# One projection burst and one transpose group per pair of heads, in an attention-plus-FFN kernel

## The chip, the core and the metric

The kernel runs on one core of one Trainium2 chip. The metric is the device time of one execution in microseconds (us). Each version is timed in several runs, and the median is compared. One further execution is recorded by the hardware profiler; its span runs from the first instruction to the last.

## The reference

A linear attention feeds a feed-forward network (FFN). All data are fp32.

```python
def phi(x):
    proj = np.einsum('bhsd,df->bhsf', x, w_phi)
    proj = proj - np.max(np.abs(proj), axis=-1, keepdims=True)
    return np.concatenate([np.exp(proj), np.exp(-proj)], axis=-1)
q_p, k_p = (phi(q), phi(k))
kv = np.einsum('bhsf,bhsd->bhfd', k_p, v)
z = np.sum(k_p, axis=2)
num = np.einsum('bhsf,bhfd->bhsd', q_p, kv)
den = np.einsum('bhsf,bhf->bhs', q_p, z)[..., None] + 1e-06
...
h = x @ w_in
g = np.maximum(h, 0.0) + alpha * np.minimum(h, 0.0)
return (g @ w_out).astype(np.float32)
```

There are 8 x 8 heads of 576 tokens with 64 dimensions, and 128 projected features, so phi has 256. The FFN sees 4608 tokens, 512 model dimensions and 2048 hidden ones.

## The kernel before

Two heads at a time form a pair, 32 pairs in all, numbered 0 to 31. One head lies on partitions 0 to 63, the other on 64 to 127. A pair goes through these steps, each a function inside `attention_units`:

- `project(0)` (L307) projects the first 512 tokens of k, 16 matmuls with a 64-row contraction into a two-bank PSUM tile `pj`. `project(1)` does the tails (the last 64 tokens of k and of q share a tile, one small PSUM tile `pl` for each head) and then the first 512 tokens of q into `pj`. There is one `pj` buffer. VectorE (DVE) follows with a maximum (L311, tile `m`) and a subtraction (L312, tile `t`) for each piece; these two are called the shift of that piece.
- `k_exp` takes exp of both signs on ScalarE (ACT): `xk` (L325) of the 512 tokens, `k` (L320) of the tail.
- `k_z` (L365) sums k features by multiplying with ones, `k_acc` (L348) accumulates `kv`, both into one PSUM bank `kv`. `kv_out` (L375) copies it to `ks`.
- `kv_turn` (L380, three transposes into `kt`) and `q_turn` (L391 for the tails, L394 for the rest, ten transposes into `qt`) turn kv and q; `kv_copy` (L384) and `q_exp` (L402, L404) bring them to SBUF as `sf` and `qf`.
- `den` (L431) and `num` (L413) multiply `qf` with `sf` into the PSUM tiles `d` and `n`; ACT copies them out (L441, L424). The denominator goes through DRAM to be inverted on DVE (L450) and spread, GpSimd multiplies, and the result is stored to `x_d`.

The FFN goes in two passes over the hidden dimension. The first five of sixteen hidden blocks are done beside the attention, one chunk of 512 tokens at a time (`ffn1_units`): four steps of three matmuls (L503 to L505) make one hidden block `h`; ACT makes `r` and `g` from it (L235, L236), DVE joins them (L240), ACT casts `gh` (L123), DVE makes the rest `gl` (L127), and steps of three matmuls (L509 to L511) multiply down into `o`, which ACT copies to `os` (L554). The second pass follows once all attention is done, at about 630 us. Weights come as 64-bit words and are decoded in blocks during the attention: ACT scales (L173), DVE splits in four instructions (L181 to L184, tiles `aw` and `ew`), GpSimd adds, ACT casts (L123, `raww`), GpSimd subtracts.

The order of the instructions on TensorE (PE), SyncE, DVE and ACT is written by hand: every step is a unit with a place on a time axis, on which one pair takes 1.0, and all units are emitted sorted by place. `places(i)` holds the places of pair i relative to i, `decode_at` those of the weight decoding, `ffn1_units` those of the FFN. The engines run their instructions in that order; places are no times. Pairs 0 to 8 (`ZP = 9`) are called early here. No FFN lies beside them but at the end, and z is made by 20 PE instructions from `xk`. For the later pairs DVE adds up z (L334, L338, L341), and 10 or 11 FFN steps lie within each. A cycle begins at the tail projection of its pair, and the start of that instruction is called T0.

Of the kernel before, what the change touches and what calls it, by code (L numbers as in the profile page):

```python
# [8 lines left out]
F32 = mybir.dt.float32  # L9
# [3 lines left out]
ALU = mybir.AluOpType  # L13
# [3 lines left out]
P = 128  # L17
# [22 lines left out]
WA = (0.0040, 0.50)  # L40
# [17 lines left out]
def places(i):  # L58
# [3 lines left out]
        ld=-1.90,  # L62
        lv=-0.80,
        p=(-0.9955 if early else -0.993, 0.0),
        ke=(-0.26, 0.0011),
        ks=(0.0015, 0.0022, 0.0026),
        kz=1.0002,
        ka=1.0012,
        ko=1.0025,
        kr=1.10,  # L70
        kc=1.16,
        q=(1.34, 1.50, 1.20),
        qe=(1.46, 1.62, 1.28),
        d=2.0004,
        ds=2.0008,
        n=2.005,
        s=2.0055,
# [31 lines left out]
def fused_kernel(ctx: ExitStack, tc: tile.TileContext, kq, v, w_phi, w_in, w_out, alpha, out):  # L109
# [111 lines left out]
    def decode_at(t, blk):  # L221
        return [(t + (WT if t < TL else WL)[k], lambda u=u: u(*blk, WN)) for k, u in stages.items()]
# [32 lines left out]
    ps_m = ps_m_.enter_context(tc.tile_pool(name="ps_m", bufs=3, space=PSUM))  # L255
# [5 lines left out]
    ps_pj = att.enter_context(tc.tile_pool(name="ps_pj", bufs=1, space=PSUM))  # L261
# [3 lines left out]
    pool.memset(ones, 1.0)  # L265
    k4buf = []
# [5 lines left out]
    def attention_units(i):  # L272
# [12 lines left out]
        def project(ch):  # L285
            t = c["t", ch] = wk.tile([P, 2, 4 + ch, FD], F32, tag=f"t{ch}", name=f"t{i}_{ch}", bufs=1 + ch)
            dst, out, js = {}, [], [0, 1, 2, 3]
            if ch:
                js = [4] + js
                for h in range(2):  # L290
                    p1 = ps_m.tile([P, 1, 1, FD], F32, tag="m", name=f"pl{i}_{h}")
                    dst[h, 4] = p1[:, 0, 0]
                    out.append((slice(h, h + 1), slice(4, 5), p1))
            if ch == 0 and i < 2:
                for h in range(2):
                    p1 = psf.tile([P, 1, 4, FD], F32, tag="f", name=f"pj{i}_{ch}_{h}")
                    dst.update({(h, j): p1[:, 0, j] for j in range(4)})
                    out.append((slice(h, h + 1), slice(0, 4), p1))
            else:
                p2 = ps_pj.tile([P, 2, 4, FD], F32, tag="pj", name=f"pj{i}_{ch}")  # L300
                dst.update({(h, j): p2[:, h, j] for h in range(2) for j in range(4)})
                out.append((slice(0, 2), slice(0, 4), p2))
            for j in js:
                for h in range(2):
                    hs = slice(h * D, (h + 1) * D)
                    ts = slice((4 * ch + j) * P, (4 * ch + j + 1) * P)
                    pe.matmul(dst[h, j], lhsT=c["raw"][hs, ts], rhs=w_sb[hs], start=True, stop=True)  # L307
            for n, (hs, js, src) in enumerate(out):
                nh, nj = hs.stop - hs.start, js.stop - js.start
                m = wk.tile([P, nh, nj], F32, tag="m", name=f"m{i}_{ch}_{n}", bufs=4)  # L310
                dve.tensor_reduce(m, src, axis=AX.X, op=ALU.max, apply_absolute_value=True)  # L311
                dve.tensor_tensor(  # L312
                    t[:, hs, js], src, m.unsqueeze(3).broadcast_to([P, nh, nj, FD]), op=ALU.subtract
                )
# [28 lines left out]

        def k_acc():
# [11 lines left out]
        def k_z():  # L356
            c["kv"] = ps_kv.tile([P, 3, FD], F32, tag="kv", name=f"kv{i}")
# [15 lines left out]
        def kv_out():  # L373
            c["ks"] = st.tile([P, 3, FD], F32, tag="ks", name=f"ks{i}", bufs=1)
            act.copy(c["ks"], c["kv"])  # L375

        def kv_turn():
            ps = c["kt"] = ps_m.tile([P, 3, P], F32, tag="m", name=f"kt{i}")
# [422 lines left out]
```

## Time and profile before

| | us |
|---|---|
| median of 3 runs | 1140.08 (1139.42 to 1140.46) |
| profiled execution, its own time | 1140.04 |
| its span | 1138.2 |
| PE busy | 1114.4 (98%) |
| DVE busy | 634.0 (56%) |
| ACT busy | 561.1 (49%) |

1.84 us of the profiled execution lie outside its span. Lines L12 are those of the kernel. In a timeline row stand start, time of the instruction or of the group, engine, line, operation, result tile <- operand tiles, shapes, count, and in brackets the idle time ahead of it with what ended it. On PE the form `64*128` is the part of the array in use (rows by columns). Matmuls overlap, so what one costs is read from the start of it to the start of the next.

### The profile page before, as it was taken

The numbers are of one execution on the slowest core, as the hardware profiler recorded it, in microseconds if no ns is written. First come the engines' busy times: TensorE is split into PE (matmuls) and PEld (weight loads), VectorE is DVE, ScalarE is ACT, GpSimd is POOL, SyncE is SP. The second block draws the span as 40 slices with busy tenths as digits, with TensorE's granted clock in tenths as the row PEclk, the third lists the DMA queues.
The fourth block names the chain that finished last, engine by engine and source line by source line (L and its number), as shares of the span: only waits on it lengthen the run. The fifth ranks groups of instructions, "written<-read, shape, count | busy, mean of one in ns | idle before, by whom it ended". The sixth has DMA issues, their size and how long they took to land.

```text
span 1138.2 us, 18351 instructions
## 1 busy us (share of the span) xinstructions
PE 1114.4 (98%) x7232; PEld 865.2 (76%) x7232; DVE 634.0 (56%) x978; ACT 561.1 (49%) x1149; POOL 213.9 (19%) x219
## 2 busy tenths in 40 slices
PE   6999999999999999999999999999999999999998
PEld 5766767777777777677778788888888888888886
DVE  7888957798687777836861342424242333333322
ACT  4777656666666765664543333333333333433332
POOL 1345332322424142243542000000000000000000
PEclk9999999999999999999999999999999999999999
DMA  5467264555556365466627030303030302112021
GB/s 190 147 186 219 68 194 143 172 164 183 162 167 195 99 211 167 146 202 219 227 65 246 32 111 1 111 1 111 1 111 1 111 1 75 37 33 79 1 74 37
DMA packets 74101, 133.68 MB, mean 117 GB/s; under 512 B 14624, under 2 KB 24480, under 8 KB 73376
## 3 DMA queue, kind: packets, MB, share of 16 engines
q1 hardware_dynamic: 71712, 122.48, 33.7%
q0 software_dynamic: 2016, 9.96, 2.5%
q8 instruction: 57, 0.93, 0.3%
q14 instruction: 28, 0.23, 0.1%
q10 hardware_dynamic: 288, 0.07, 0.0%
HBM read 93.92 MB, written 38.42 MB: 116 GB/s over the span
## 4 chain that ended last, share of the span: by engine, by line
PE 88%; DVE 6%; DMA 4%; ACT 2%; issue 1%; SPq 0%; DVEq 0%; ACTq 0%
PE h L503 11%; PE h L505 11%; PE h L504 11%; PE po L511 8%; PE po L509 8%; PE po L510 8%; PE kv L348 6%; PE n L413 5%; PE pj L307 5%; PE o L511 3%; PE o L509 3%; PE o L510 3%; PE d L431 2%; PE qt L394 2%; DMA xr<-x_d 2%; PE kv L365 1%
## 5 line engine op out<-in xcount | busy, mean ns | idle before, releaser
L240 DVE SCALAR_TENSOR_TENSOR g<-r,aln,g 128x512 f32<-128x512 f32 x144 | 111.7, 775 | 307.1 <-ACT g L236 306.9
L235 ACT ACTIVATE r<-h 128x512 f32<-128x512 f32 x144 | 86.5, 601 | 293.3 <-PE h L505 293.2
L127 DVE TENSOR_TENSOR gl<-g,gh 128x512 fp32r<-128x512 f32 x144 | 104.7, 727 | 67.6 <-ACT gh L123 67.1
L123 ACT CAST gh<-g 128x512 fp32r<-128x512 f32 x144 | 90.0, 625 | 85.6 <-DVE g L240 85.6
L236 ACT ACTIVATE g<-h 128x512 f32<-128x512 f32 x144 | 86.0, 598 | 1.0 <-DMA part_d<-os 1.0
L509 PE MATMUL po<-gh,wd 128*128 128x512 f32 x216 | 84.6, 392 | 0.7 <-ACT gh L123 0.7
L510 PE MATMUL po<-gh,wd 128*128 128x512 f32 x216 | 84.7, 392 | 0.0
L511 PE MATMUL po<-gl,wd 128*128 128x512 f32 x216 | 84.5, 391 | 0.0
L311 DVE TENSOR_REDUCE m<-pj 128x8 f32<-128x1024 f32 (+1 forms) x66 | 78.2, 1185 | 10.4 <-PE pj L307 10.3
L307 PE MATMUL pj<-w_sb,raw 64*128 64x128 f32 x1024 | 73.2, 283 | 9.8 <-DMA w_sb<-w_phi_dram 4.6
L307 PEld LDWEIGHTS pj<-w_sb,raw 64*128 64x128 f32 x1024 | 64.1, 192 | 23.3 <-issue 15.6
L189 POOL TENSOR_TENSOR aw<-ew,aw 128x256 f32<-128x256 f32 x64 | 56.6, 885 | 128.6 <-DVE ew L184 128.6
L312 DVE TENSOR_TENSOR t<-pj,m 128x1024 f32<-128x1024 f32 (+1 forms) x66 | 78.7, 1192 | 2.3
L509 PE MATMUL o<-gh,w 128*128 128x512 f32 x180 | 76.0, 422 | 2.6 <-ACT os L554 2.4
L463 POOL TENSOR_TENSOR s<-s,rr 128x576 f32<-128x576 f32 x32 | 48.5, 1517 | 145.3 <-DMA rr<-rec_d 127.7
L503 PE MATMUL h<-xh,w 128*128 128x512 f32 x180 | 75.8, 421 | 0.0
L511 PE MATMUL o<-gl,w 128*128 128x512 f32 x180 | 71.7, 399 | 3.6 <-DVE gl L127 3.4
L404 ACT ACTIVATE qf<-qt 128x512 f32<-128x512 f32 x128 | 68.4, 615 | 6.3 <-PE qt L394 6.3
L511 PE MATMUL po<-gl,w 128*128 128x512 f32 x180 | 69.7, 390 | 1.4 <-DVE gl L127 1.4
L505 PE MATMUL h<-xl,w 128*128 128x512 f32 x180 | 70.7, 393 | 0.0
L510 PE MATMUL o<-gh,w 128*128 128x512 f32 x180 | 70.6, 392 | 0.0
L504 PE MATMUL h<-xh,w 128*128 128x512 f32 x180 | 70.5, 392 | 0.0
(105 smaller groups left out, 2402.6 us busy)
## 6 DMA issues: line engine op xcount, KB each, us to landing
xr<-x_d SPq DMA_DIRECT2D x18, 1024.0 KB
raw<-kq_dram SPq DMA_DIRECT2D x31, 576.0 KB
v<-v_dram SPq DMA_DIRECT2D x32, 320.0 KB
w_d<-raww SPq DMA_DIRECT2D x38, 256.0 KB
rr<-rec_d SPq DMA_DIRECT2D x64, 144.0 KB
x_d<-s SPq DMA_DIRECT2D x32, 288.0 KB
part_d<-os SPq DMA_DIRECT2D x36, 256.0 KB
pt<-part_d SPq DMA_DIRECT2D x9, 1024.0 KB
```

The lines of the kernel that those rows point to most:

```text
L123: return act.copy(dst, src)
L127: return eng.tensor_tensor(dst, src, f(hi), op=ALU.subtract)
L235: act.activation(st["r"], ps, AF.Relu, scale=-1.0)
L236: act.activation(st["g"], ps, AF.Relu)
L240: dve.scalar_tensor_tensor(g, st["r"], aln[:, ff : ff + 1], g, op0=ALU.mult, op1=ALU.add)
L307: pe.matmul(dst[h, j], lhsT=c["raw"][hs, ts], rhs=w_sb[hs], start=True, stop=True)
L503: pe.matmul(ps, lhsT=wt[0][:, ws], rhs=xh, start=n == 0, stop=False)
L504: pe.matmul(ps, lhsT=wt[1][:, ws], rhs=xh, start=False, stop=False)
L505: pe.matmul(ps, lhsT=wt[0][:, ws], rhs=xl, start=False, stop=n == NK - 1)
L509: pe.matmul(ps, lhsT=wt[2][:, ws], rhs=gh, start=first, stop=False)
L510: pe.matmul(ps, lhsT=wt[3][:, ws], rhs=gh, start=False, stop=False)
L511: pe.matmul(ps, lhsT=wt[2][:, ws], rhs=gl, start=False, stop=last)
```

## The change

On PE the pieces of a pair's cycle get another order. The three projections stand together at its start as one burst of nine tiles: the tails, the first 512 tokens of k of the next pair, the first 512 tokens of q. Behind them come, in later pairs, kv, the numerator, the denominators and z; in early pairs the denominators, z, kv and the numerator. All transposes of a pair form one group, in later pairs behind the first FFN step, where before they stood in four places between FFN steps: three of kv, two of the q tails, eight of q. The q tails are turned from the lower 64 partitions alone (`t[D:P]`), 64 columns each, beside the turned kv in one PSUM bank `kq`.

PSUM is divided anew: `pj` has two buffers, shared by the projections, the turned q and the numerator, where `ps_m` has one buffer instead of three. The tail of the first head is projected into a free column of the bank in which kv of the pair before is accumulated afterwards (`kvb`). The shifts are units of their own (`shift`), in the order tail of head 0, next pair's k, tail of head 1, q. On ACT, `xk` moves to place -0.45, `qf` is made by one instruction for each sign in later pairs, and the numerator is copied out by one. The second decode block of an early pair is taken right behind the first. A split whose place falls late in a cycle (over .88) moves behind the shifts of the next one.

The core of the diff:

```diff
-WA = (0.0040, 0.50)
+WA = (0.0040, 0.0046)
...
-        ld=-1.90,
+        ld=-1.9988,
...
-        p=(-0.9955 if early else -0.993, 0.0),
-        ke=(-0.26, 0.0011),
...
+        p=(-0.9994 if i < ZP + 3 else -0.9998, 0.0004),
...
+        ke=(-0.45, 0.0014),
...
     def decode_at(t, blk):
-        return [(t + (WT if t < TL else WL)[k], lambda u=u: u(*blk, WN)) for k, u in stages.items()]
+        us = []
+        for k, u in stages.items():
+            at = t + (WT if t < TL else WL)[k]
+            if k == "split" and ZP < at < TL and at % 1 > 0.88:
+                at = int(at) + 1.0009
+            us.append((at, lambda u=u: u(*blk, WN)))
+        return us
...
-    ps_m = ps_m_.enter_context(tc.tile_pool(name="ps_m", bufs=3, space=PSUM))
+    ps_m = ps_m_.enter_context(tc.tile_pool(name="ps_m", bufs=1, space=PSUM))
...
-    ps_pj = att.enter_context(tc.tile_pool(name="ps_pj", bufs=1, space=PSUM))
+    ps_pj = att.enter_context(tc.tile_pool(name="ps_pj", bufs=2, space=PSUM))
...
+        def shift(n):
+            ch, hs, js, src = c["p", n]
...
+            dve.tensor_reduce(m, src, axis=AX.X, op=ALU.max, apply_absolute_value=True)
+            dve.tensor_tensor(
+                c["t", ch][:, hs, js], src, m.unsqueeze(3).broadcast_to([P, nh, nj, FD]), op=ALU.subtract
+            )
...
+        def project(ch, js):
+            if len(js) == 1:
+                kvb[i] = ps_kv.tile([P, 4, FD], F32, tag="kv", name=f"kv{i}")
+                pl = ps_m.tile([P, 4, FD], F32, tag="m", name=f"pl{i}")
+                dst = [kvb[i][:, 3:4], pl[:, 0:1]]
...
+            else:
+                dst = ps_pj.tile([P, 2, 4, FD], F32, tag="pj", name=f"pj{i}_{ch}")
...
+        def kv_bank():
...
+            c["kv"] = kvb[i + 1]
...
+        def q_turn():
+            for g in range(2):
+                pe.transpose(c["kq"][:, 3, g * D : (g + 1) * D], c["t", 1][D:P, g, 0, :], ident[D:P, D:P])
...
         def num():
+            c["n"] = ps_pj.tile([P, 2, 512], F32, tag="pj", name=f"n{i}")
...
-        for n in range(2):
-            us.append((at["p"][n], lambda n=n: project(n)))
+        us.append((at["p"][0], lambda: project(0, range(4))))
+        us.append((1.0008, kv_bank))
+        us.append((at["pl"], lambda: project(1, range(1))))
+        us.append((at["p"][1], lambda: project(1, range(1, 5))))
+        for n in range(4):
+            us.append((at["sh"][n], lambda n=n: shift(n)))
```

The order of PE at the start of pair 21's cycle, before: `pl21` are its tails, `pj21_1` its q, `pj22_0` the k of pair 22; `kv20` belongs to pair 20, `d19` and `n19` to pair 19.

```order
L307 MATMUL pl21_0_3868<-w_sb_73,raw21_3578 128x128
L307 MATMUL pl21_1_3869<-w_sb_73,raw21_3578 128x128
L307 MATMUL pj21_1_3870<-w_sb_73,raw21_3578 128x128 x8
L365 MATMUL kv20_3890<-z20_3727,ones_119 32x128 x4
L431 MATMUL d19_3895<-qf19_3793,sf19_3772 32x288 x8
L348 MATMUL kv20_3890<-xk20_3653,v20_3591 64x256 x8
L348 MATMUL kv20_3890<-k4_0_121,v20_3591 64x256 x2
L413 MATMUL n19_0_3928<-qf19_3793,sf19_3772 64x288 x4
L413 MATMUL n19_1_3933<-qf19_3793,sf19_3772 64x288 x4
L307 MATMUL pj22_0_3942<-w_sb_73,raw22_3767 128x128 x8
L503 MATMUL h1_3_2_3850<-xh1_3_3571,w2_92 128x512
L504 MATMUL h1_3_2_3850<-xh1_3_3571,w2_92 128x512
```

The same place now; `kv21` is the bank that takes the first tail of pair 21 and then kv of pair 20.

```order
L320 MATMUL kv21_3740<-w_sb_73,raw21_3420 128x128
L320 MATMUL pl21_3741<-w_sb_73,raw21_3420 128x128
L320 MATMUL pj22_0_3744<-w_sb_73,raw22_3605 128x128 x8
L320 MATMUL pj21_1_3753<-w_sb_73,raw21_3420 128x128 x8
L359 MATMUL kv21_3740<-xk20_3527,v20_3491 64x256 x8
L359 MATMUL kv21_3740<-k4_0_121,v20_3491 64x256 x2
L432 MATMUL n19_3798<-qf19_3667,sf19_3662 64x288 x8
L449 MATMUL d19_3807<-qf19_3667,sf19_3662 32x288 x8
L375 MATMUL kv21_3740<-z20_3643,ones_119 32x128 x4
L525 MATMUL h1_3_2_3728<-xh1_3_3462,w2_92 128x512
L526 MATMUL h1_3_2_3728<-xh1_3_3462,w2_92 128x512
L527 MATMUL h1_3_2_3728<-xl1_3_3463,w2_92 128x512
```

The projection of pair 22's k stood behind the numerator and now stands ahead of kv; the denominators and z stood ahead of kv and now stand behind the numerator.

The order of DVE ahead of that burst, before: L240 joins an FFN block, L450 inverts, L127 makes the rest, L181 to L184 split a weight block, L311 and L312 are the shifts.

```order
L240 SCALAR_TENSOR_TENSOR g1_3_0_3800<-r1_3_0_3799,aln_76,g1_3_0_3800 128x512
L450 RECIPROCAL r9_18_3847<-d9_18_3791 128x9
L127 TENSOR_TENSOR gl1_3_0_3854<-g1_3_0_3800,gh1_3_0_3834 128x512
L240 SCALAR_TENSOR_TENSOR g1_3_1_3840<-r1_3_1_3839,aln_76,g1_3_1_3840 128x512
L181 TENSOR_SCALAR aw8_0_0_3832<-aw8_0_0_3832 128x256
L182 SCALAR_TENSOR_TENSOR aw8_0_0_3832<-raww8_0_0_3786,aw8_0_0_3832 128x256
L183 TENSOR_SCALAR ew8_0_0_3857<-aw8_0_0_3832 128x256
L184 SCALAR_TENSOR_TENSOR ew8_0_0_3857<-raww8_0_0_3786,ew8_0_0_3857 128x256
L311 TENSOR_REDUCE m21_1_0_3881<-pl21_0_3868 128x1
L312 TENSOR_TENSOR t21_1_3867<-pl21_0_3868,m21_1_0_3881 128x128
L311 TENSOR_REDUCE m21_1_1_3884<-pl21_1_3869 128x1
L312 TENSOR_TENSOR t21_1_3867<-pl21_1_3869,m21_1_1_3884 128x128
```

DVE now, at the same place (L248 is the join, L468 the reciprocal, L129 the rest, L300 and L301 the shifts):

```order
L248 SCALAR_TENSOR_TENSOR g1_3_0_3691<-r1_3_0_3690,aln_76,g1_3_0_3691 128x512
L468 RECIPROCAL r9_18_3725<-d9_18_3684 128x9
L129 TENSOR_TENSOR gl1_3_0_3732<-g1_3_0_3691,gh1_3_0_3715 128x512
L248 SCALAR_TENSOR_TENSOR g1_3_1_3721<-r1_3_1_3720,aln_76,g1_3_1_3721 128x512
L300 TENSOR_REDUCE m21_0_3763<-kv21_3740 128x1
L301 TENSOR_TENSOR t21_1_3762<-kv21_3740,m21_0_3763 128x128
L300 TENSOR_REDUCE m22_2_3767<-pj22_0_3744 128x8
L301 TENSOR_TENSOR t22_0_3766<-pj22_0_3744,m22_2_3767 128x1024
L300 TENSOR_REDUCE m21_1_3770<-pl21_3741 128x1
L301 TENSOR_TENSOR t21_1_3762<-pl21_3741,m21_1_3770 128x128
L300 TENSOR_REDUCE m21_3_3773<-pj21_1_3753 128x8
L301 TENSOR_TENSOR t21_1_3762<-pj21_1_3753,m21_3_3773 128x2x512
```

The split of weight block 8 has moved from ahead of the shifts to behind them, the shift of pair 22's k stands between the two tails, and the join of FFN block 1 (`g1_3_1`) is still ahead of all of them.

The order of ACT ahead of that burst, before: L235 and L236 make r and g, L404 the q features, L123 casts, L173 scales, L325 makes `xk`.

```order
L235 ACTIVATE r1_3_0_3799<-h1_3_0_3758 128x512
L236 ACTIVATE g1_3_0_3800<-h1_3_0_3758 128x512
L404 ACTIVATE qf19_3793<-qt19_0_3803 128x512 x2
L404 ACTIVATE qf19_3793<-qt19_1_3818 128x512 x2
L123 CAST raww7_1_256_3634<-aw7_1_256_3667 128x256
L173 ACTIVATE aw8_0_0_3832<-raww8_0_0_3786 128x256
L123 CAST gh1_3_0_3834<-g1_3_0_3800 128x512
L235 ACTIVATE r1_3_1_3839<-h1_3_1_3810 128x512
L236 ACTIVATE g1_3_1_3840<-h1_3_1_3810 128x512
L325 ACTIVATE xk21_3843<-t21_0_3745 128x1024 x2
L441 ACTIVATE ds19_3904<-d19_3895 128x288
L320 ACTIVATE k4_1_123<-t21_1_3867 64x256 x2
```

ACT now (L243 and L244 are r and g, L423 the q features, L125 the casts, L175 the scale, L331 `xk`):

```order
L419 ACTIVATE qf19_3667<-kq19_3647 128x2x64 x2
L423 ACTIVATE qf19_3667<-qt19_3653 128x2x512
L243 ACTIVATE r1_3_0_3690<-h1_3_0_3639 128x512
L244 ACTIVATE g1_3_0_3691<-h1_3_0_3639 128x512
L423 ACTIVATE qf19_3667<-qt19_3653 128x2x512
L331 ACTIVATE xk21_3706<-t21_0_3582 128x1024 x2
L125 CAST raww7_1_256_3521<-aw7_1_256_3552 128x256
L175 ACTIVATE aw8_0_0_3713<-raww8_0_0_3679 128x256
L125 CAST gh1_3_0_3715<-g1_3_0_3691 128x512
L243 ACTIVATE r1_3_1_3720<-h1_3_1_3697 128x512
L244 ACTIVATE g1_3_1_3721<-h1_3_1_3697 128x512
L326 ACTIVATE k4_1_123<-t21_1_3762 64x256 x2
```

`xk21`, which stood behind r and g of FFN block 1, now stands ahead of them, and so ahead of the cast and scale of the weights and of `gh` too.

121 lines of the change are left out of this document (56 added, 65 removed).

## The prediction

> **What bounds the kernel now.** I read the page first, then the groups of waits of PE, then the timelines of PE, DVE and ACT around single pairs.
>
> ```profile
> PE 1114.4 (98%) x7232; PEld 865.2 (76%) x7232; DVE 634.0 (56%) x978; ACT 561.1 (49%) x1149; POOL 213.9 (19%) x219
> ...
> PE o L509 <- ACT os L554: 2.4, 1, 2.4
> PE d L431 <- ACT qf L404: 1.0, 2, 0.7
> ```
>
> PE is busy 98% of the span, so a change can gain only where PE does the same work in less time or waits less, and it loses where PE is made to wait. What its work costs stands in the timeline of PE around pair 21, whose cycle begins at T0 = 309.31 (start, length, line):
>
> ```profile
> 308.99 0.39 PE L505 MATMUL h<-xl,w 128*128 128x512 f32 x1
> 309.31 0.49 PE L307 MATMUL pl<-w_sb,raw 64*128 64x128 f32 x4
> 309.63 1.06 PE L307 MATMUL pj<-w_sb,raw 64*128 64x128 f32 x16
> 310.62 0.42 PE L365 MATMUL kv<-z,ones 128*32 128x128 f32 x8
> ...
> 311.95 1.95 PE L348 MATMUL kv<-xk,v 128*64 128x256 f32 x16
> ...
> 314.16 2.11 PE L413 MATMUL n<-qf,sf 128*64 128x288 f32 x16
> 316.20 1.16 PE L307 MATMUL pj<-w_sb,raw 64*128 64x128 f32 x16
> 317.29 0.50 PE L503 MATMUL h<-xh,w 128*128 128x512 f32 x1
> ...
> 318.08 0.49 PE L380 MATMUL kt<-ident,ks 128*128 128x128 f32 x3
> ...
> 319.11 0.38 PE L391 MATMUL qt<-ident,t 128*128 128x128 f32 x2
> ...
> 320.72 0.60 PE L394 MATMUL qt<-ident,t 128*128 128x128 f32 x4
> ...
> 321.85 0.60 PE L394 MATMUL qt<-ident,t 128*128 128x128 f32 x4
> ```
>
> From start to start the tails take 0.32 us, the q projection 0.99, z and denominators 1.33, kv 2.21, the numerator 2.04, the next k projection 1.09. Nowhere here does PE wait. The four-transpose group and the FFN step behind it take 1.13 (320.72 to 321.85), the three-transpose group and its step 1.03 (318.08 to 319.11), so a transpose is 0.10 to 0.11 and a step 0.69 to 0.71, and a group has no price of its own.
>
> DVE is 56% busy, but in bursts. Its timeline around the same T0:
>
> ```profile
> 309.59 0.75 DVE L240 SCALAR_TENSOR_TENSOR g<-r,aln,g 128x512 f32<-128x512 f32 x1 [0.29 <-ACT g L236]
> 310.26 0.29 DVE L181 TENSOR_SCALAR aw<-aw 128x256 uint32<-128x256 uint32 x1
> ...
> 311.78 0.28 DVE L311 TENSOR_REDUCE m<-pl 128x1 f32<-128x128 f32 x1
> 312.10 0.29 DVE L312 TENSOR_TENSOR t<-pl,m 128x128 f32<-128x128 f32 x1
> 312.31 0.28 DVE L311 TENSOR_REDUCE m<-pl 128x1 f32<-128x128 f32 x1
> ...
> 312.83 1.21 DVE L311 TENSOR_REDUCE m<-pj 128x8 f32<-128x1024 f32 x1
> 314.08 1.22 DVE L312 TENSOR_TENSOR t<-pj,m 128x1024 f32<-128x1024 f32 x1
> ```
>
> A join (L240) takes 0.67, a split of weights 1.52, the shift of one tail 0.53, that of a 1024-column piece 1.25 and 1.22. I call S the start of the first tail's shift; here it is T0 + 2.47, since a join and a split lie ahead of it, and PE doesn't care. It begins to care at pair 29:
>
> ```profile
> 442.08 0.49 PE L307 MATMUL pl<-w_sb,raw 64*128 64x128 f32 x4
> ...
> 446.93 2.11 PE L413 MATMUL n<-qf,sf 128*64 128x288 f32 x16
> 449.19 1.16 PE L307 MATMUL pj<-w_sb,raw 64*128 64x128 f32 x16
> 445.61 0.28 DVE L311 TENSOR_REDUCE m<-pl 128x1 f32<-128x128 f32 x1
> 447.91 1.22 DVE L312 TENSOR_TENSOR t<-pj,m 128x1024 f32<-128x1024 f32 x1
> ```
>
> S is T0 + 3.53 there. The subtraction that frees the only `pj` buffer ends at 449.13, and the next projection starts 0.06 later, 2.26 behind the numerator's start instead of 2.04. So before, the kernel bore an S of about T0 + 3.3 without loss.
>
> **PE's own work.** In later pairs the next k projection moves beside the q projection. A projection behind another kind of matmul costs 1.09, and 0.99 is what q takes with only the exit from this form; so an entry and an exit, 0.10 each, go away: -0.20 a pair. The transposes gather in one group, which by the above saves nothing; but the two tails are now turned on 64 rows, in the midst of 128-row transposes. No such transpose is in the trace. From below, they cost half a transpose each and no change of form: -0.1 a pair. From above, they take a whole 0.11 each, and the array changes form twice, at the exit and entry prices that the projections show (leaving transposes +0.09, into 64 rows +0.10, out +0.10, into transposes +0.05): +0.35. For the first, the leaving price, early pairs show it:
>
> ```profile
> 52.85 0.55 PE L380 MATMUL kt<-ident,ks 128*128 128x128 f32 x3
> ...
> 54.42 0.49 PE L307 MATMUL pl<-w_sb,raw 64*128 64x128 f32 x4
> ...
> 63.42 0.55 PE L380 MATMUL kt<-ident,ks 128*128 128x128 f32 x3
> ```
>
> The 13 transposes there last 1.57 up to the first projection, 0.15 more than 13 times 0.109. I take +0.30, near the upper end, because the projections are the nearest row: the same 64 rows, beside the same transposes. The Trainium skill, "TensorEngine Tiling (Array Packing)", section "Key Properties", speaks against this edit too: changing the tiling mode, not just the tile, drains the TensorE. By that rule the sum would be the one with +0.30, and the rows with 0.15 and 0.10 agree; its own "Overview" promises up to twice the speed for small dimensions, which would be the lower end.
>
> A later pair so costs +0.10, and 20 of them cost +2.0 (pairs 9 to 11 start up and end in waits, below). An early cycle (63.42 less 52.85 is 10.57) saves the same 0.20, another 0.14 since no projection parts kv from the numerator, and pays 0.28: -0.06, and -0.4 for seven.
>
> **The waits that come.** The new order asks DVE for more in less time. kv is accumulated in the bank that holds the first tail, so it waits for that tail's subtraction; the numerator takes the `pj` buffer of the next k, so it waits for that shift too. On PE, kv stands at T0 + 2.20 (0.32 + 0.89 + 0.99) and the numerator at T0 + 4.41. On DVE the first subtraction ends at S + 0.61 and next k's at S + 0.53 + 1.25 + 1.22 = S + 3.00; with 0.06 to PE, kv is late by S - 1.53 and the numerator, all told, by S - 1.35. What S may be without loss falls from T0 + 3.3 to T0 + 1.35. Behind the waiting matmul stands all of PE, in order.
>
> Now S itself, worked out for pair 21. ACT ahead of it before:
>
> ```profile
> 304.40 0.60 ACT L235 ACTIVATE r<-h 128x512 f32<-128x512 f32 x1 [0.95 <-PE h L505]
> 304.90 0.59 ACT L236 ACTIVATE g<-h 128x512 f32<-128x512 f32 x1
> 305.38 2.07 ACT L404 ACTIVATE qf<-qt 128x512 f32<-128x512 f32 x4
> 307.28 0.45 ACT L123 CAST raww<-aw 128x256 fp32r<-128x256 f32 x1
> 307.58 0.48 ACT L173 ACTIVATE aw<-raww 128x256 f32<-128x256 f32 x1
> 307.91 0.66 ACT L123 CAST gh<-g 128x512 fp32r<-128x512 f32 x1
> 308.42 0.65 ACT L235 ACTIVATE r<-h 128x512 f32<-128x512 f32 x1
> ```
>
> r and g take 0.98 together, 2048 columns of exp 1.90, the cast 0.30, the scale 0.33, `gh` 0.51. After the change FFN block 0 ends six steps (4.14) ahead of the last one, whose end starts 0.32 ahead of T0; its r starts 0.43 later, at T0 - 4.03. Then ACT has, in the order that the diff gives it: r and g to -3.05, one sign of q to -2.10, `xk21` to -0.20, the cast to +0.10, the scale to +0.43, `gh` to +0.94, r and g of block 1 to +1.92, done at +2.02. Only then can DVE join them, to +2.75, and the shift stands behind that join. S is 2.75, the wait 1.40. Before, `xk` stood behind that r and g; taking it earlier is what makes the join late, while the moved split takes 1.52 off DVE.
>
> The same count for the other later pairs gives S of 0.5 to 1.0 in most, which costs nothing, and 3.16 at pair 14, 2.0 at 16, 2.77 at 17, 2.14 at 25, 1.9 at 26, 3.07 at 29 and 4.70 at 30 (there `xk30` stands ahead of cast, scale and split, and the split ahead of the shift). Less 1.35 each that is 1.81 + 0.65 + 1.40 + 1.40 + 0.79 + 0.55 + 1.72 + 3.35 with pair 21's 1.40 in it. At pair 10 the denominators follow the burst at once and need the second tail's shift: 0.75. Together +12.4. These are estimates from the rows above, and each chain of eight or nine terms can be off by 0.5; the bounds are 4 (only the worst three remain, shortened) and 14.
>
> **The waits that go.** They are those behind crowded DVE or ACT queues:
>
> ```profile
> 471.73 0.50 PE L511 MATMUL o<-gl,w 128*128 128x512 f32 x1 [1.57 <-DVE gl L127]
> 205.48 0.50 PE L511 MATMUL o<-gl,w 128*128 128x512 f32 x1 [0.34 <-DVE gl L127]
> ```
>
> These two and the 0.22 at pair 29 go, since shifts of k no longer stand between FFN joins and rests there: -2.1. The 1.0 of the denominators for `qf` falls at pairs 8 and 9, where the order changes throughout: -1.0, with bounds of -1.9 and +1. The 2.4 for `os` stays, since it hangs on a transfer; reckoned from its own T0 the restart is later by +0.35. The loads that SyncE now issues slightly earlier lie 4 us or more ahead of their users, and `ks`, which the transpose group waits for, comes 0.05 to 0.1 ahead of it by the same count; both at nothing, the second with a price of about 0.3 a pair if ACT is late.
>
> **The sum.** -0.4 early, -1.0 and +0.35 at the change-over, +2.0 for the later pairs' matmuls, +12.4 and -2.1 for waits: +11.25 against the profiled execution's 1140.04 (its span and 1.84 us outside). It lies 0.04 under the median, so I forecast 1151.3 us.
>
> **Rivals.** (1) The 64-row transposes change no form. Then a pair costs 0.30 less (27 pairs in all, 8.0): 1143.3. For it speaks only that the trace has no such instruction. Chance 0.08. (2) The late joins do not come, because ACT is idle half of the time and a few chains end sooner than I count; below S = 1.35 nothing waits. Sum without the 12.4: 1138.9, with a third of it 1143. This is the one that ends not slower, at S - T0 under 1.35 in all pairs but two. Against it speaks pair 21, where every link was read from rows. Chance 0.18, of which 0.08 faster and 0.10 the same. (3) Both of these: 1131 to 1135. Chance 0.14, since a tail without its drain and lighter ACT queues both shorten the chain. (4) ACT's copy `ks` comes behind the transposes' place in most pairs, as the numerator and denominators are copied ahead of it; at 0.3 a pair 6 us more: 1157. Chance 0.08. That the change does not do what it says can't be: PE's order shows the burst and the group.
>
> My forecast has 0.52, on its own 1145 to 1154. The range of 1138 to 1156 leaves out rival 3 and the upper half of 4. A measurement here tells 0.2% (2.3 us) from no change: faster 0.22 (rival 3 and 0.08 of 2), the same 0.10, slower 0.68.
>
> **What would show it.** In the profile after, PE's waits should have kv and the numerator waiting for the subtraction, about 12 us in eight or nine places, the largest over 3 at pair 30, and a join should end right ahead of the first shift in each. In a late cycle without a wait the burst to z should last 7.8 us (7.98 before), and the 13 transposes about 1.7 (1.43 before), with a gap around the two tails. Wrong I am if kv follows the projections without a gap at pairs 14, 21 and 29, or if the tails follow their neighbours at 0.11 or less.

## The result and the profile after

The changed kernel takes 1158.87 us (median of 4, 1154.48 to 1161.66) against 1140.27 before: a ratio of 1.0158 with an interval of 1.0132 to 1.0183. A second comparison gave 1159.16 against 1141.72, 1.0157 (1.0139 to 1.0175). It is slower, as forecast, by 18.6 us instead of 11.2, and lies above the range.

Two things have to be kept apart. The profiled execution took 1154.48 us with a granted clock (the share of its full speed that TensorE was given) of 1.000; the other three showed 0.992 to 0.996 and took 1156.24 to 1161.66. So 14.4 us of the difference are there at full clock, and some 4 us more in the median come with a lower clock.

Where the 14.4 lie is read from T0 of single pairs in the two traces. Up to pair 10 the changed kernel gains 1.36 us (T0 at 115.67 instead of 117.03; forecast -1.4). That this is so near the forecast is luck: the cycle of pair 7 is 1.48 longer than before, with a wait of 1.57 for `ks` that was forecast at nothing, and the next cycle is 2.69 shorter, where -1.0 was forecast; in the second comparison's trace the gain is 0.31. From pair 10 to pair 31 it loses 14.64 (490.47 instead of 477.19; forecast +12.65). Behind pair 31 it loses another 0.76, and 0.40 outside the span, where nothing was forecast.

The page of the changed kernel, and what its PE waited for:

```profile
PE 1117.9 (97%) x7232; PEld 869.3 (75%) x7232; DVE 629.2 (55%) x974; ACT 552.7 (48%) x1069; POOL 207.4 (18%) x219
...
PE kv L359 <- DVE t L301: 13.8, 11, 3.5
...
PE d L449 <- DVE t L301: 2.1, 3, 1.3
PE kq L393 <- ACT ks L385: 1.6, 1, 1.6
...
PE n L432 <- DVE t L301: 0.2, 1, 0.2
```

A row gives the time in all, the number of waits and the longest. kv now waits for the shift of the first tail, at 11 places, and the three waits of the denominators are for a shift too. This is the wait that the prediction named. Pair 21, whose T0 is 314.72 here, on PE:

```profile
314.72 0.37 PE L320 MATMUL kv<-w_sb,raw 64*128 64x128 f32 x1
...
315.05 1.95 PE L320 MATMUL pj<-w_sb,raw 64*128 64x128 f32 x32
318.12 1.95 PE L359 MATMUL kv<-xk,v 128*64 128x256 f32 x16 [1.12 <-DVE t L301]
319.90 0.60 PE L359 MATMUL kv<-k,v 128*64 128x256 f32 x4
320.61 2.16 PE L432 MATMUL n<-qf,sf 128*64 128x288 f32 x16
```

On DVE at the same place, a join and then the shifts:

```profile
316.79 0.75 DVE L248 SCALAR_TENSOR_TENSOR g<-r,aln,g 128x512 f32<-128x512 f32 x1 [0.29 <-ACT g L244]
317.46 0.28 DVE L300 TENSOR_REDUCE m<-kv 128x1 f32<-128x128 f32 x1
317.78 0.29 DVE L301 TENSOR_TENSOR t<-kv,m 128x128 f32<-128x128 f32 x1
...
319.23 1.23 DVE L301 TENSOR_TENSOR t<-pj,m 128x1024 f32<-128x1024 f32 x1
```

And on ACT ahead of that join:

```profile
312.62 2.02 ACT L331 ACTIVATE xk<-t 128x1024 f32<-128x1024 f32 x2
314.52 0.41 ACT L125 CAST raww<-aw 128x256 fp32r<-128x256 f32 x1
...
315.65 0.61 ACT L243 ACTIVATE r<-h 128x512 f32<-128x512 f32 x1
```

S is 317.46 - 314.72 = 2.74 (forecast 2.75), `xk` starts at T0 - 2.10 as counted, and the wait is 1.12 ahead of kv. The numerator starts 2.49 behind kv instead of 2.21, since it waits for the next shift in turn; only 0.10 of these 0.28 us is recorded as idle. All told it is 1.5 late, where 1.40 was forecast. The projections are one burst; without the wait kv would start at 316.93.

At pair 19, which the forecast had among those whose S costs nothing, a split stood ahead of the shift and waited for its scale, and the scale stood behind `xk` on ACT:

```profile
281.44 0.29 DVE L183 TENSOR_SCALAR aw<-aw 128x256 uint32<-128x256 uint32 x1 [3.24 <-ACT aw L175]
...
282.97 0.28 DVE L300 TENSOR_REDUCE m<-kv 128x1 f32<-128x128 f32 x1
```

```profile
279.01 2.00 ACT L331 ACTIVATE xk<-t 128x1024 f32<-128x1024 f32 x2
280.92 0.41 ACT L175 ACTIVATE aw<-raww 128x256 f32<-128x256 f32 x1
```

S is 2.15 there (T0 at 280.82), and the numerator 0.88 late.

The group of transposes of an undisturbed pair, between two FFN steps:

```profile
306.85 0.50 PE L393 MATMUL kq<-ident,ks 128*128 128x128 f32 x3
307.28 0.33 PE L401 MATMUL kq<-ident,t 64*128 64x64 f32 x2
307.54 1.09 PE L412 MATMUL qt<-ident,t 128*128 128x128 f32 x8
308.39 0.48 PE L525 MATMUL h<-xh,w 128*128 128x512 f32 x1
```

It takes 1.54 us (forecast about 1.7), 0.43 for three transposes ahead of the tails, where 0.33 would do. From T0 to the end of z such a cycle takes 7.79 us (forecast 7.8).

### The profile page after: what moved, and what is told of

Its sections match the earlier page's. It is cut to its first block, busy times and chain, and to the rows that moved or that the text cites. A ratio compares the mean times of both kernels' runs of the same rounds, so it can differ in the third digit from the quotient of the medians.

```text
span 1152.3 us, 18237 instructions
## 1 busy us (share of the span) xinstructions
PE 1117.9 (97%) x7232; PEld 869.3 (75%) x7232; DVE 629.2 (55%) x974; ACT 552.7 (48%) x1069; POOL 207.4 (18%) x219
## 4 chain that ended last, share of the span: by engine, by line
PE 75%; ACT 8%; DVE 6%; DMA 6%; issue 2%; SPq 1%; POOL 0%; DVEq 0%; ACTq 0%; POOLq 0%
PE h L525 9%; PE h L527 9%; PE h L526 9%; PE po L533 8%; PE po L531 8%; PE po L532 8%; PE kv L359 5%; PE n L432 5%; PE d L449 3%; PE o L531 2%; PE qt L412 2%; PE o L533 2%; PE pj L320 2%; PE o L532 2%; ACT qf L423 2%
## 5 line engine op out<-in xcount | busy, mean ns | idle before, releaser
L248 DVE SCALAR_TENSOR_TENSOR g<-r,aln,g 128x512 f32<-128x512 f32 x144 | 111.0, 771 | 323.5 <-ACT g L244 323.1
L243 ACT ACTIVATE r<-h 128x512 f32<-128x512 f32 x144 | 86.8, 603 | 288.1 <-PE h L527 288.1
L129 DVE TENSOR_TENSOR gl<-g,gh 128x512 fp32r<-128x512 f32 x144 | 102.2, 710 | 74.9 <-ACT gh L125 74.6
L125 ACT CAST gh<-g 128x512 fp32r<-128x512 f32 x144 | 90.1, 626 | 79.7 <-DVE g L248 79.7
L244 ACT ACTIVATE g<-h 128x512 f32<-128x512 f32 x144 | 86.2, 598 | 1.6 <-DMA part_d<-os 1.6
L301 DVE TENSOR_TENSOR t<-pj,m 128x1024 f32<-128x1024 f32 x64 | 78.4, 1225 | 3.8 <-ACT xk L331 0.4
L300 DVE TENSOR_REDUCE m<-pj 128x8 f32<-128x1024 f32 x64 | 77.8, 1216 | 3.4 <-PE pj L320 3.4
L359 PE MATMUL kv<-xk,v 128*64 128x256 f32 x512 | 62.3, 385 | 13.8 <-DVE t L301 13.8
L531 PE MATMUL o<-gh,w 128*128 128x512 f32 x180 | 73.1, 406 | 1.1 <-ACT os L576 1.0
L320 PE MATMUL pj<-w_sb,raw 64*128 64x128 f32 x1024 | 67.8, 284 | 6.1 <-DMA w_sb<-w_phi_dram 4.3
L525 PE MATMUL h<-xh,w 128*128 128x512 f32 x180 | 72.8, 404 | 0.0
L532 PE MATMUL o<-gh,w 128*128 128x512 f32 x180 | 70.2, 390 | 0.0
L526 PE MATMUL h<-xh,w 128*128 128x512 f32 x180 | 70.2, 390 | 0.0
L532 PE MATMUL po<-gh,w 128*128 128x512 f32 x180 | 70.0, 389 | 0.0
L531 PE MATMUL po<-gh,w 128*128 128x512 f32 x180 | 70.0, 389 | 0.0
```

The costliest lines, as they stand in the source:

```text
L125: return act.copy(dst, src)
L129: return eng.tensor_tensor(dst, src, f(hi), op=ALU.subtract)
L243: act.activation(st["r"], ps, AF.Relu, scale=-1.0)
L248: dve.scalar_tensor_tensor(g, st["r"], aln[:, ff : ff + 1], g, op0=ALU.mult, op1=ALU.add)
L320: pe.matmul(dst[h][:, n], lhsT=c["raw"][hs, o : o + P], rhs=w_sb[hs], start=True, stop=True)
L359: pe.matmul(c["kv"][h * D : (h + 1) * D, 0:2], lhsT=c["v"][:, tp, h, :], rhs=c["x", ch][:, :, h, j, :], start=tp == 0, stop=tp == NV - 1,)
```

## The experiments

All ratios are to the kernel before, run on the same chip in the same call.

| run | median us | ratio (95% interval) |
|---|---|---|
| after_again | 1159.16 | 1.0157 (1.0139 to 1.0175) |
| xk_late | 1153.11 | 1.0112 (1.0094 to 1.0131) |
| splits_behind | 1155.25 | 1.0124 (1.0109 to 1.0140) |
| xk_last_splits | 1152.66 | 1.0099 (1.0081 to 1.0117) |
| t0_two_buffers | 1146.07 | 1.0040 (1.0026 to 1.0053) |
| t0_tails_in_burst | 1140.58 | 0.9996 (0.9981 to 1.0011) |
| tails_128 | 1159.72 | 1.0161 (1.0143 to 1.0179) |
| before_tails_64 | 1145.80 | 1.0038 (1.0023 to 1.0053) |
| before_three_waits | 1155.93 | 1.0127 (1.0107 to 1.0148) |
| best_raw_three_wa | 1176.16 | 1.0314 (1.0300 to 1.0328) |
| best_raw_three | 1143.86 | 1.0028 (1.0018 to 1.0038) |
| raw_three_buffers | 1163.69 | 1.0199 (1.0186 to 1.0212) |
| t0_raw_behind | 1147.37 | 1.0047 (1.0028 to 1.0067) |
| t0_raw_tails | 1142.41 | 1.0010 (0.9997 to 1.0023) |
| before_raw_ahead | 1142.47 | 1.0010 (0.9997 to 1.0023) |
| xk_last_splits_xh | 1153.46 | 1.0117 (1.0095 to 1.0139) |
| weights_early | 1146.14 | 1.0050 (1.0036 to 1.0063) |
| weights_early_xh | 1150.38 | 1.0081 (1.0062 to 1.0101) |

**The clock: after_again and before_three_waits.** The first is the changed kernel once more.

> The changed kernel once more, unaltered, beside the next three and beside the kernel before. Its profiled execution had the full clock, a time of 1154.5 us and a longest wait of PE of 3.6 us at pair 30; the granted clock of three other executions was 0.992 to 0.996, and they took 1156 to 1162. Theory (the clock falls behind the one long wait): here again some executions lie below 1.0 and the median is 1156 to 1160. Rival (the clock of that chip was low by chance): all executions at 1.0 and 1154.5, or the kernel before falls too.

It took 1157.49 to 1161.62 at 0.994 to 0.995. Its profiled execution fell to half the clock at the end of the wait at pair 30. First the stretch of the wait and what followed, then the same in the execution at full clock (the last but two column is the granted clock):

```profile
476.55 3.68 PE L359 MATMUL kv<-xk,v 128*64 128x256 f32 x16 [3.53 <-DVE t L301]
480.02 1.07 PE L359 MATMUL kv<-k,v 128*64 128x256 f32 x4
...
475.50:482.40 6.90, 5.85 (x28) 3.22 (x30) 6.73 (x11) 0.72 (x2) 2.13 (x2) 0.51 0.66 205
```

```profile
475.87 1.95 PE L359 MATMUL kv<-xk,v 128*64 128x256 f32 x16 [3.53 <-DVE t L301]
477.65 0.60 PE L359 MATMUL kv<-k,v 128*64 128x256 f32 x4
...
474.80:481.70 6.90, 5.73 (x60) 3.29 (x60) 6.73 (x11) 1.38 (x4) 2.13 (x2) 1.00 0.68 206
```

The same wait of 3.53 us, and the same 16 matmuls take 3.47 us at half clock and 1.78 at full. The cycle took 22.93 us instead of 20.41, so 2.5 us more with the same wait. before_three_waits makes such waits in the kernel before, where nothing else changes:

```diff
-                dve.tensor_reduce(m, src, axis=AX.X, op=ALU.max, apply_absolute_value=True)
+                for _ in range(6 if (ch, n) == (1, 2) and i in (18, 22, 27) else 1):
+                    dve.tensor_reduce(m, src, axis=AX.X, op=ALU.max, apply_absolute_value=True)
```

> The kernel before with the reduction of one shift repeated five more times on DVE (same values) at pairs 18, 22 and 27, so that PE waits there 0.52 + 3.57 + 6.25 - 6.89 = 3.4 us each time, 10.3 us in all. Theory (a wait of over 3 us lets the clock fall to half for one or two spans of 3.4 us): most executions show the half clock behind some of these waits, each taking 1.7 to 3.4 us more; time 1151 to 1158. Rival (the clock falls for a reason outside the kernel): clock as in the kernel before beside it, and 1149.5 to 1152.

```profile
343.02 1.23 PE L307 MATMUL pj<-w_sb,raw 64*128 64x128 f32 x16 [3.48 <-issue]
...
344.00:347.40 3.40, 3.40 (x13) 2.58 (x10) 3.16 (x5) 1.75 (x6) 1.22 (x1) 0.50 0.10 31
347.40:350.80 3.40, 3.40 (x21) 2.82 (x20) 3.23 (x8) 1.48 (x5) 0.00 (x0) 1.00 0.86 248
```

All three waits were 3.48 us, and behind each the clock was half for 3.4 us; the three cycles lost 4.95, 4.93 and 5.12 us. So a wait of that length, where the clock fell behind it, cost itself and 1.45 to 1.64 us more. 13 executions of the kernel before in that call showed 0.995 to 1.000, those of this kernel 0.994 to 0.995. A fourth half-clock stretch of that execution, at 153 us, stands at the end of a wait of 2.65 us for `os` that the edit doesn't make. The rival is out: three waits were put in, and each brought the low clock. It is not certain for each wait, as the pair above shows. In all profiled executions taken together, behind the first 25 us, 19 of 22 waits of 3.0 us or more had a half clock at or behind their end, and 10 of 20 of those between 1.8 and 3.0; three more such stretches stood behind waits of 1.8 or less. The Trainium skill, "TensorE: Matmul & The Clock Gate", Part 1, tells of a gate that halves the clock after an idle window of some 3.4 us that runs freely; the length of the half-clock stretches (3.4 and 6.8) and the chance in it agree here, while waits of 1.8 to 2.9 us, shorter than the window, were enough here in several cases.

**What makes the shift late: xk_late, splits_behind, xk_last_splits, t0_two_buffers.**

```diff
-        ke=(-0.45, 0.0014),
+        ke=(-0.26, 0.0014),
```

> One place put back: xk on ScalarE at -0.26 as before the change, behind r, g and the weights' casts. Theory (the joins and splits are late because xk stands ahead of them): the first shift of pairs 14, 16, 17, 19, 21, 23, 25 and 29 comes 1.9 us earlier, under T0 + 1.35, and their waits go, 1.7 + 1.7 + 1.3 + 0.7 + 1.3 + 1.0 + 0.7 + 1.6 = 10 us; pairs 26 and 30 keep theirs. At full clock 1144.5. Rival (DVE itself is too full in these cycles): waits stay within 30% and the time is above 1151. As pair 30 keeps its 3.6 us wait, the theory of the clock expects some executions below 1.0 here too.

Half right. Counting the idle time ahead of kv and of the numerator together, pairs 19, 21 and 25 lost their waits, 16 and 17 kept 0.72 and 0.89, but 23 rose from 0.90 to 1.57 and 29 from 1.51 to 2.02, and 14 stayed at 1.58: at -0.26 `xk` stood ahead of r and g, of `gh` or of the scale of the next block there, so the queue was as long. The wait of pair 30, expected to stay at 3.63, was 2.44. From pair 10 to pair 30 its profiled execution lost 8.9 us on the kernel before, where the changed kernel's lost 12.6: 3.7 won, not 10.

```diff
-            if k == "split" and ZP < at < TL and at % 1 > 0.88:
-                at = int(at) + 1.0009
+            if k in ("split", "add") and ZP < t < TL and (t + 0.25) % 1 < 0.2501:
+                at = max(at, int(t + 0.25) + (0.0009 if k == "split" else 0.05))
```

> The splits of weights that still stood ahead of the shifts at pairs 16, 19, 23, 26 and 30 are moved behind them, with their additions. Theory: the waits at 16, 19, 23 and 26 go (1.7 + 0.7 + 1.0 + 0.7) and the one at 30 falls from 3.6 to about 2.3, 5.4 us in all, 1149 at full clock. The theory of the clock expects every execution at 1.0, as no wait over 2.5 us is left behind the first 13 us; the rival that the clock falls from the number of waits, or by chance, expects some below 1.0 as in the changed kernel.

The waits at 16, 19, 23 and 26 went, and that at 30 fell from 3.63 to 2.12, as expected; behind 106 us the clock was 1.00 throughout. But the expectation on the clock failed: the four executions stood at 0.994 to 0.997. In the profiled one the half clock came behind a wait of 2.67 us for `ks` at 98.8 us, which this edit doesn't touch, and at pair 11 it was 5.4 us behind the kernel before, where the changed kernel was 0.5 behind. So the median fell by 3.9 us only.

xk_last_splits has that edit and `xk` last:

```diff
-        ke=(-0.45, 0.0014),
+        ke=(-0.45 if early else 0.0012, 0.0014),
```

> The changed kernel with two things in later pairs: xk on ScalarE behind everything that stands ahead of the burst (place 0.0012 of its own pair instead of -0.45), and every split behind the shifts. With xk at -0.26 the waits only moved, since xk then stood ahead of the cast, scale or r and g of the next block instead. Theory: all first shifts of pairs 10 to 30 start before T0 + 1.35, so that the waits of kv, numerator and denominators there go, 14.9 us of recorded idle time and 0.25 more at each of 11 places, 17 us in all: 1137 to 1138 at full clock, and no fall of the clock in the later pairs. Rival (DVE and ACT are simply too full in the new order): waits come back at other places, above 1146.

The rival holds: the waits came back elsewhere, nine for the numerator, 6.1 us. Pair 22 on DVE, ACT and PE:

```profile
333.16 1.21 DVE L300 TENSOR_REDUCE m<-pj 128x8 f32<-128x1024 f32 x1
336.20 1.22 DVE L301 TENSOR_TENSOR t<-pj,m 128x1024 f32<-128x1024 f32 x1 [1.83 <-ACT xk L331]
...
334.17 2.00 ACT L331 ACTIVATE xk<-t 128x1024 f32<-128x1024 f32 x2
...
337.57 1.68 PE L432 MATMUL n<-qf,sf 128*64 128x288 f32 x12 [1.70 <-DVE t L301]
```

The next k's subtraction writes `t`, which has one buffer, and waits until `xk` has read it. With its projection in the burst, that subtraction starts at T0 + 2.8 in a cycle of the changed kernel without a wait, where it started at T0 + 9.4 in most cycles before (T0 + 9.9 at pair 21), and so `xk` has to be early, and so the joins are late. The one buffer ties them. t0_two_buffers adds a second one to that kernel:

```diff
-                ... name=f"t{i}_{ch}", bufs=1 + ch)
+                ... name=f"t{i}_{ch}", bufs=2)
```

> The kernel with xk last and the splits behind the shifts, and a second buffer for t of the first 512 tokens of k. In the kernel without it the shift of the next k stood waiting for xk, which had to read the one buffer first (9 waits of the numerator, 6.1 us, one of the denominators of 2.1, two of kv, 1.1). Theory: with the second buffer xk may stand last and these waits go, about 9 to 11 us: 1141 to 1143. Rival (DVE is too full in the new order whatever stands ahead): waits of 5 us or more are left, and the time stays above 1147.

```profile
PE kq L393 <- ACT ks L385: 3.9, 3, 2.0
...
PE kv L359 <- DVE t L301: 0.7, 1, 0.7
```

Of 16 us of waits of kv, numerator and denominators for shifts one of 0.7 was left, beside pieces of 0.12 or less. From pair 12 to 31 the kernel then needs 1.4 us more than the kernel before, in place of 13.1. The median, 1146.07, is 3 us over the 1141 to 1143 that were expected: the profiled execution lost 5.2 us between pairs 7 and 11, with 3.9 us of waits for `ks` and two half-clock stretches.

**The form of the array: before_tails_64, tails_128, t0_tails_in_burst.**

```diff
-                    pe.transpose(ps[:, g, :], c["t", 1][:, g, 0, :], ident)
+                    pe.transpose(ps[:, g, D:], c["t", 1][D:P, g, 0, :], ident[D:P, D:P])
```

> The kernel before with one part of the change alone: the q tails turned from 64 rows with 64 columns, at their old place. In the changed kernel the transposes ahead of them last 0.204 instead of 0.109, the first two behind them 0.10 longer together, and a tail takes 0.11 as before. Theory (two changes of form): 0.2 a pair, 6 us, 1145 to 1147. Rival (smaller transposes are cheaper or equal): 1139 to 1141.

```profile
54.09 0.55 PE L380 MATMUL kt<-ident,ks 128*128 128x128 f32 x3
54.57 0.33 PE L391 MATMUL qt<-ident,t 64*128 64x64 f32 x2
54.83 1.09 PE L394 MATMUL qt<-ident,t 128*128 128x128 f32 x8
55.85 0.49 PE L307 MATMUL pl<-w_sb,raw 64*128 64x128 f32 x4
```

The group takes 1.76 instead of 1.57 (0.48, 0.26 and 1.02 where 0.38, 0.22 and 0.97 stood). Each early cycle without a wait is 0.195 longer, each such later one 0.24, and the median 1145.80, 4.4 over the kernel before in that call. The edit alone is slower.

tails_128 turns the tails over all rows by plain matmuls with the last 64 columns of the identity.

```diff
-                pe.transpose(c["kq"][:, 3, g * D : (g + 1) * D], c["t", 1][D:P, g, 0, :], ident[D:P, D:P])
+                pe.matmul(c["kq"][:, 3, g * D : (g + 1) * D], lhsT=c["t", 1][:, g, 0, :], rhs=ident[:, D:P], ...)
```

> The two q tails are turned by matmuls over all 128 rows with the last 64 columns of the identity, so that the 13 transposes keep one form of the array; nothing else changes. Theory (the change of form costs 0.1 to 0.15 a pair, 1.54 instead of 1.43 us for the group): 4 us less over 32 pairs, 1150.5 at full clock. Rival (the group's time is its work, no form is paid for): within 1 us of the changed kernel.

A cycle gained 0.01, not 0.1 to 0.15. It doesn't tell the two apart: a plain fp32 matmul took two passes (four entries in the trace for two tails), and the two added ones (0.20) made up for the two changes of form. t0_tails_in_burst is t0_two_buffers with 64 rows kept, but it puts the tails of pairs 9 to 30 where that form rules anyway, behind the next pair's tail projections:

```diff
+        if ZP <= i < NPAIR - 1:
+            us.append((1.0002, lambda: tail_turn(plb[i + 1][:, 1])))
```

> As the one before, and the q tails of pairs 9 to 30 turned one cycle later, between the tail projections and the projections, whose form of 64 rows they share; the group of transposes has eleven left. Theory of the form (two changes cost 0.2 a pair): 22 times 0.2 = 4.4 us under the kernel before it in this list. Rival (the tails' cost goes along): within 1.5 us of it.

```profile
310.22 0.28 PE L402 MATMUL pl<-ident,t 64*128 64x64 f32 x2
...
318.64 0.55 PE L393 MATMUL kq<-ident,ks 128*128 128x128 f32 x3
319.03 1.04 PE L417 MATMUL qt<-ident,t 128*128 128x128 f32 x8
319.82 0.48 PE L532 MATMUL h<-xh,w 128*128 128x512 f32 x1
```

A cycle without a wait is now 0.27 shorter than before the change, in place of 0.05; the 0.22 a pair are in the main the two changes of form. Start to start a tail takes 0.06 in the burst, where it took 0.11 between the 128-row transposes: the two add 0.17 to the burst, and the group falls from 1.54 to 1.18. The median is 5.5 us under t0_two_buffers and level with the kernel before: 0.9996 (0.9981 to 1.0011). So the repairs take back the loss, and no gain is shown.

**Early pairs: the rest.** best_raw_three_wa (below) puts the second weight block back at 0.50:

```diff
-WA = (0.0040, 0.0046)
+WA = (0.0040, 0.50)
```

> The same with the second weight block of early pairs back at half a cycle (0.50). If taking both blocks at once crowds ACT in early cycles: another 1 to 2 us off at 85 to 115 us. Otherwise within 1 us of the one above, or slower, since the splits then stand ahead of a shift.

```profile
PE d L454 <- DVE t L301: 29.9, 8, 4.2
```

32 us slower. With the split of the second block ahead of the shift, the denominators wait 3.1 to 4.2 us in eight early cycles, and the clock fell to 0.985. The prediction had no word on this part of the change; it is what the new early order rests on, 32.3 us against best_raw_three.

What was not settled is why the transposes wait for `ks` between 80 and 115 us, 1 to 4 us in all, differently in each execution. ACT in t0_tails_in_burst, ahead of `ks`:

```profile
91.59 0.62 ACT L125 CAST xh<-xr 128x512 fp32r<-128x512 f32 x1 [2.78 <-DMA xr<-x_d]
...
96.29 0.43 ACT L175 ACTIVATE aw<-raww 128x256 f32<-128x256 f32 x1 [1.75 <-DMA raww<-w_out_dram]
...
98.05 0.45 ACT L385 COPY ks<-kv 128x384 f32<-128x384 f32 x1
```

Two entries that wait for transfers stand ahead of it. The next kernels each moved one thing or another, and none won:

> As the one before, and the casts of the first FFN chunk (xh on ScalarE), which wait for their transfer with the copy ks queued behind them, 5 us later (0.5 of a pair). Theory (the transposes' waits for ks at 85 to 108 us, 0 to 3.3 us from execution to execution, are that cast's wait for its transfer): those waits go, the spread between executions falls under 3 us, and the median is 1 to 2 us under the kernel without this. Rival (ks is late for another reason): waits and spread stay.

Casts of the chunk later (`FX0`, the places of the four casts of a chunk, in xk_last_splits):

```diff
-FX0 = (1.80, 1.35, 0.95, 0.45)
+FX0 = (1.30, 1.10, 0.85, 0.45)
```

The waits for `ks` were 2.7 and 4.2, behind the scale of a weight block that waited 4.0 and 4.2 us for its load; the longest was 3.1 without the edit.

The loads of `raw` back at their old place, in t0_two_buffers and in t0_tails_in_burst:

```diff
-        ld=-1.9988,
+        ld=-1.90,
```

> As the first of these four, with the loads of raw back at -1.90, behind the store of the reciprocals on SyncE's queue instead of ahead of it. In the changed kernel the spread of the reciprocals is issued 3.1 to 3.7 us behind their store in early pairs, 1.5 us in the kernel before, and the load of the first FFN chunk 2.8 us later. Theory (the 576 KB load ahead delays the small store, and everything behind it up to the casts that hold up ks): spread 1.5 us behind the store, load of the chunk 2 us earlier, the waits of transposes for ks at 80 to 115 us (0.9 to 4.2 us in all) down to 1 or less, 2 to 3 us faster. Rival (the load is then too late for the projection burst): as much is lost in waits of projections for raw.

> Both of these together. If the theories hold, the sum: 6 to 7 us under the first of the four, 1135 to 1137, which is below the kernel before the change.

The waits for `ks` fell to 1.1 and to none, but the projections waited 3.0 and 4.3 us for `raw`. That was the rival, and neither kernel was faster for it.

Three buffers of `raw`, loaded earlier, in the changed kernel and in t0_tails_in_burst:

```diff
-RAW_BUFS = 2
+RAW_BUFS = 3
...
-        ld=-1.9988,
+        ld=-2.45,
```

> The changed kernel with a third buffer for raw and its loads half a cycle earlier (-2.45), clear of the reciprocals' store and early enough for the burst; nothing else. Theory (the load just ahead of the store delays it, and with it the first FFN chunk, whose casts hold up ks): the chunk's load is issued 2 us earlier, near 82, the waits for ks at 80 to 115 us fall to 1 us or less, and the median is 2 to 4 us under the changed kernel's 1159. Rival (they come from the weights' decoding on ACT or the burst's order): waits for ks as before, within 1.5 us.

> The repaired kernel (two buffers for t, xk last, splits behind, tails in the burst) with the third buffer of raw and its earlier loads. If the loads are the cause of the waits for ks: 3 us under the repaired kernel's 1140.6, 1137.5, below the kernel before by 0.3%. If not: 1139.5 to 1141.5.

The waits for `ks` stayed (3.8 and 6.4 us in all), so they come without a load of `raw` just ahead of the store too.

The converse in the kernel before, its load at the changed kernel's place:

```diff
-        ld=-1.90,
+        ld=-1.9988,
```

> The kernel before with the loads of raw moved from -1.90 to -1.9988 alone, ahead of the reciprocals' store as in the changed kernel. Theory: the spread is issued about 2 us later behind its store in early pairs, the first chunk's load near 84 instead of 81.6, and 1 to 3 us are lost at 85 to 110. Rival: within 0.7 us of the kernel before.

For the three stores between 59 and 82 us, the spread of the inverted denominators is issued 2.9 to 3.4 us behind its store instead of 1.5 to 2.3; for the one at 50 us it is 1.7 instead of 2.5. But the chunk's load is issued at 82.26, near its 81.56 before and not at 84; the denominators wait 2.1 instead of 1.0, and the ratio of 1.0010 (0.9997 to 1.0023) leaves it open whether anything is lost.

Loads of the weight blocks 0.4 of a pair earlier in t0_tails_in_burst, then with the casts of the chunk later as well:

```diff
+            if k == "load" and 3 < t < 11.5:
+                at -= 0.40
...
-FX0 = (1.80, 1.35, 0.95, 0.45)
+FX0 = (1.12, 0.90, 0.60, 0.25)
```

> The repaired kernel (1140.6, level with the kernel before) with the loads of the weight blocks of pairs 3 to 10 issued 0.4 of a pair earlier. If the scale's wait for its load is what delays ks: ScalarE has no wait over 0.5 us for weights before 115 us, the waits for ks fall from 3.5 us to that which the cast of the chunk leaves, about 1.5, and the median is 1 to 2 us lower. If the cast alone does it: within 0.7 us of 1140.6.

> The same, and the casts of the first FFN chunk behind ks of pair 7 (1.12 pairs ahead of the chunk's start instead of 1.80). If the two are all that delays ks: no wait for ks over 0.5 us behind 25 us, 3 us under the repaired kernel, 1137.5, which would be 0.3% under the kernel before. If ks is late for another reason, or the chunk then starts late: 1139.5 or more.

The scale then waited for GpSimd instead, up to 5.2 us in the first kernel (2.79, 3.85, 4.12, 0.79 and 5.21) and up to 7.0 in the second. By the code, GpSimd's subtraction of an earlier block reads the buffer that the scale writes; that this is the tie wasn't tried. One wait was traded for another, and both kernels are slower. So what is left at 80 to 115 us stays open.

## Why the prediction was right and wrong

**The bound and the wait** were right: PE waits for shifts behind joins and splits, kv first, then the numerator. S was forecast at 3.16, 2.77, 2.75, 2.14, 3.07 for pairs 14, 17, 21, 25, 29 and measured at 3.09, 2.73, 2.74, 2.11, 3.02. In all five a join ends right ahead of the first shift.

**The step that failed is the sum of the waits, "Together +12.4".** It counts how late the numerator comes. By the same measure (its start behind T0, less the 4.42 of a cycle without a wait) the changed kernel lost 16.0 us in pairs 14 to 30, 1.76 at pair 11, and 1.34 in the denominators' wait at pair 10: 19.1 in all. Most of what was missed lies at four places. At 16, 19 and 23 a split stood ahead of the shift and waited for a scale that stood behind `xk`: 1.81 instead of 0.65 at 16, and 0.88 and 1.14 at 19 and 23, which were counted among those that cost nothing. Pair 11 was not in the list; there the wait for `os`, which was to stay at 2.4 and cost 0.35 more, fell to 0.32, so that the two nearly cancel. Smaller parts are 0.5 at pair 30 (S 5.15 instead of 4.70), 0.6 at pair 10 and 0.3 at pair 26.

The second fault is of the same sum: "the bounds are 4 and 14" took a wait for its own length, and one of 3.5 us can cost up to 2.5 more by the half clock. The execution at full clock, 1154.5, lies inside the range, since the errors of the waits, of `os` and of PE's own work go both ways, which is luck too. The median lies outside, among executions at a lower clock. In the one of these that was profiled, after_again's, the half clock behind the wait of pair 30 cost 2.5; the executions that set the median have no trace, so how much of their loss stands behind that wait, and how much behind the waits for `ks` at 80 to 115 us, is not shown.

**PE's own work** erred to the other side. The join of the projections saved its 0.20 (7.79 from T0 to the end of z instead of 7.98), but the tails cost 0.15 more, not 0.30; before_tails_64, where they were changed alone, puts the two changes of form at 0.19 to 0.24. An undisturbed later cycle is 0.03 to 0.06 shorter, where +0.10 was forecast: 3 us over 20 pairs. Of the rivals the first was wrong (the form is paid for), the second too, and with them the third; the fourth (a late `ks` in most pairs) holds at a few early pairs only. The early cycles gained 0.155 each, not 0.06.

**Priced at nothing**, and wrong so: "`ks`, which the transpose group waits for, comes 0.05 to 0.1 ahead of it". It holds in the later pairs, but for 0.12 at pair 24; at 80 to 115 us it fails by up to 3.5 us (1.57 in the profiled execution), differently in each execution.

## What to carry to other kernels

When a change moves a consumer forward, write down for each engine how late its producer may be before and after: here the first shift might start at T0 + 3.3 before and T0 + 1.35 after, and that one difference held most of the result. A buffer that is reused once a cycle ties the places of its readers to its next writer; look for it before moving either. A step in another array form belongs beside others of that form: that was worth 0.22 us a pair. And a PE wait of some 3 us mostly cost more than its length.

## What was not expected of the hardware

- Behind PE waits of 3 us or more the clock was half for 3.4 or 6.8 us in 19 of 22 cases, and in 10 of 20 behind waits of 1.8 to 3.0. A half-clock stretch of 3.4 us cost 1.45 to 1.64 us beside the wait, the one of 6.8 us that was compared 2.5.
- Between 128-row transposes one of 64 rows and 64 columns took the 0.11 us, start to start, of one with 128, and two of them made the pair 0.19 to 0.24 longer. Among 64-row projections they took 0.06 each, start to start, and 0.17 the two, less than the 0.22 of two 128-row ones.
